# Block attention with decay and a gated FFN on one Trainium2 core: q of the first two batches moves to the casting DMA queue, the first tables are made in another order, and the scores of block 2 stand later in the order

## The chip, the cores and the metric

The kernel runs on one core of a Trainium2 chip. The metric is the device time of one execution in microseconds (us), as a median over several executions. Engines are named as in the profile: PE (TensorE matmul), PEld (its weight loads), DVE (VectorE), ACT (ScalarE), POOL (GpSimd) and SP (SyncE, which here only issues DMAs).

## The reference

Inputs are q, k, v of shape (4 batches, 8 heads, 768 positions, 64), one decay `lam` per head, and three FFN weights (512x1536, 512x1536, 1536x512), all fp32. The reference works in blocks of positions; the kernel uses blocks of 128.

```python
Dmask = np.where(rel >= 0, lam ** rel, 0)                 # inside a block
intra = (qb @ kb.T * Dmask) @ vb
inter = (qb * lam ** (pos + 1)) @ kv_state                # what earlier blocks left
out_block = intra + inter
kv_state = lam ** block * kv_state + (kb * lam ** (block - 1 - pos)).T @ vb
...
x = out (tokens x 512)
result = (sigmoid(x @ w_gate) * (x @ w_val)) @ w_out      # 3072 x 512, fp32
```

## The kernel before

The 768 positions are six blocks n = 0 to 5 of 128 positions; a block holds all four batches, so it is 512 tokens for the FFN. Everything is computed in bf16 with fp32 sums. The order on every engine is the order in which the program writes its instructions: the schedule is by hand.

**Pieces of a block.** `piece_t` gets q and k transposed, two batches at a time. For blocks 0 and 1 PE does it into PSUM (`tq`, `tk`); for blocks 2 to 5 `transpose_by_dma(n)` (line 157) issues two DMA transposes on SP, first q into `QR`, then k into `KR`, and `piece_t` is only `scale_q`. `scale_q` (line 164) is one DVE multiplication that scales q by the table `lamq` (the powers of lam) and writes `QS`. `piece_s` (line 209) forms the scores of the listed batches on PE from `KS` (a view of `KR` from block 2 on) and `QS`, in two PSUM tiles `sp` a batch; `piece_m` (line 217) multiplies one batch's scores by `mask` on DVE (two instructions); `piece_a` (lines 223, 230, 237) makes the attention output on PE and copies it to `XT` on ACT. `make_kd` (line 241) scales k on POOL, and `piece_c` (lines 249, 254, 262) updates the state `Sb`.

**FFN.** `piece_gv(n, ft)` (lines 276, 279, 282, 286) makes one of twelve column tiles: four matmuls into `gp`, a sigmoid on ACT, four matmuls into `vp`, and a DVE product `ht`. `piece_po` (line 296) makes the output, in two halves of six matmuls for each batch.

**Order.** From block 1 on, the order is a list of units: twelve `gv` units and eight `po` halves a block. `place(n, c, t, s, m, a)` hangs the pieces of the next block n behind units. For n = 2 the units are those of block 1's FFN, u = `start[1]`: the transposes behind unit u, `scale_q` of batches 0, 1 behind u+2 and of batches 2, 3 behind u+3, scores behind u+6 and u+9, the attention behind u+10 and u+13. For later blocks, scores stand behind u+4 and u+7.

**Start.** Block 0's q and k of batches 0 and 1 come by the hardware queues as fp32 into the tiles `QF` and `KF` (q on SP after `lam`, k on ACT; line 66). ACT casts k, DVE scales q by the table `qn` while casting it, and `piece_t0(b)` (line 192) transposes q and k of one batch on PE. All other loads are DMAs that cast to bf16, issued by POOL in one row: v of batches 0, 1 (line 85), the first sixth of `WG` and `WV` (`load_gv(0)`, lines 91 and 92), the table `ip1` (line 314), q and k of batches 2, 3, the next sixth of `WG` and `WV` (called WG1 and WV1 below), v of batches 2, 3, the other weights and then blocks 1 and 2. `warm(x)` (line 326) runs x idle matmuls. `load(3)` and later follow `make_kd(2)` on POOL.

**Buffers that matter here.** The `ps_at` pool has five PSUM buffers for `sp`, `op`, `tq`, `tk`, `cp`; `ps_ff` has three for `gp`, `vp`, `po`; `QS` has three.

Of the kernel before, what the change touches and what calls it, by code (L numbers as in the profile page):

```python
# [8 lines left out]
FP32 = mybir.dt.float32  # L9
BF16 = mybir.dt.bfloat16  # L10
AF = mybir.ActivationFunctionType
ALU = mybir.AluOpType
# [4 lines left out]
def kernel(  # L17
# [11 lines left out]
    nc = tc.nc  # L29

    B, H, S, D = q.shape
    C = 128
    NSTEP = S // C
    HP = H // 2
# [5 lines left out]
    NB2 = B // 2  # L40

    const = ctx.enter_context(tc.tile_pool(name="const", bufs=1))
    qkv = ctx.enter_context(tc.tile_pool(name="qkv", bufs=4))
    kdp = ctx.enter_context(tc.tile_pool(name="kdp", bufs=2))
    trsb = ctx.enter_context(tc.tile_pool(name="trsb", bufs=3))
# [3 lines left out]
    osb = ctx.enter_context(tc.tile_pool(name="osb", bufs=4))  # L49
    stp = ctx.enter_context(tc.tile_pool(name="stp", bufs=1))  # L50

    ps_at = ctx.enter_context(tc.tile_pool(name="ps_at", bufs=5, space=bass.MemoryType.PSUM))
# [6 lines left out]
    lam_bc = const.tile([128, H], FP32, tag="lam_bc")  # L59
    nc.sync.dma_start(out=lam_bc, in_=lam.partition_broadcast(128))  # L60

    QF, KF = [], []
    for lst, src, eng in ((QF, q, nc.sync), (KF, k, nc.scalar)):
        for b in range(NB2):
            t = osb.tile([128, H, D], FP32, tag="ob", name="qkf")
            eng.dma_start(out=t, in_=src[b, :, 0:C, :].rearrange("h s d -> s h d"))
            lst.append(t)

    WG = const.tile([128, NMT, DFF], BF16, tag="WG")
    WV = const.tile([128, NMT, DFF], BF16, tag="WV")  # L70
# [5 lines left out]
    Q, K, V = {}, {}, {}  # L76

    def load(n, what, b0, b1):
        sl = slice(n * C, (n + 1) * C)
        for c in what:  # L80
            lst, src = {"q": (Q, q), "k": (K, k), "v": (V, v)}[c]
            if n not in lst:
                lst[n] = qkv.tile([128, B, H, D], BF16, tag=c + "b", name=c + "b")
            t = lst[n]
            nc.gpsimd.dma_start(  # L85
                out=t[:, b0:b1],
                in_=src[b0:b1, :, sl, :].rearrange("b h s d -> s (b h) d"))
# [12 lines left out]
    Sb = stp.tile([128, B, HP, 128], BF16, tag="Sb", name="Sb")  # L100
    nc.vector.memset(Sb, 0.0)  # L101
    ident = const.tile([128, 128], BF16, tag="ident")
    jn = const.tile([128, 3], FP32, tag="jn")
    ip1 = const.tile([128, C], FP32, tag="ip1")
    tri = const.tile([128, C], FP32, tag="tri")
    for c, lst in (("q", Q), ("k", K)):
        lst[0] = qkv.tile([128, B, H, D], BF16, tag=c + "b", name=c + "b")

    for i, (base, m) in enumerate(((1, 1), (-1, -1), (C - 1, -1))):
        nc.gpsimd.iota(jn[:, i:i + 1], pattern=[[0, 1]], base=base, channel_multiplier=m,  # L110
                       allow_small_or_imprecise_dtypes=True)
    load(0, "v", 0, 2)
    make_upper_triangular(nc, tri, val=1.0, diag=True)
    make_identity(nc, ident)

    lnl = const.tile([128, H], FP32, tag="lnl")
    nc.scalar.activation(lnl, lam_bc, AF.Ln)
    qn = const.tile([128, H], FP32, tag="qn")
    nc.scalar.activation(qn, lnl, AF.Exp, scale=jn[:, 0:1])
    pk = const.tile([128, H], FP32, tag="pk")  # L120
    nc.scalar.activation(pk, lnl, AF.Exp, scale=jn[:, 1:2])

    for b in range(NB2):
        nc.scalar.copy(K[0][:, b], KF[b])
        nc.vector.tensor_tensor(out=Q[0][:, b], in0=QF[b],
                                in1=qn.unsqueeze(2).to_broadcast([128, H, D]), op=ALU.mult)
    mask = const.tile([128, HP, 2, C], FP32, tag="mask")
    lnp = const.tile([128, HP], FP32, tag="lnp")
    lamq = const.tile([128, HP, C], BF16, tag="lamq")
    kds = const.tile([128, H], FP32, tag="kds")  # L130
    dec = const.tile([128, HP], FP32, tag="dec")

    def make_mask():
        nc.vector.tensor_tensor(out=mask.rearrange("p g u c -> p (g u) c"),
                                in0=tri.unsqueeze(1).to_broadcast([128, H, C]),
                                in1=pk.unsqueeze(2).to_broadcast([128, H, C]), op=ALU.mult)

    def make_tables():
        for u in range(2):
            us = slice(u * 64, (u + 1) * 64)  # L140
            nc.scalar.activation(lnp[us, :], lam_bc[us, u::2], AF.Ln)
        for hp in range(HP):
            nc.scalar.activation(lamq[:, hp, :], ip1, AF.Exp, scale=lnp[:, hp:hp + 1])
        nc.scalar.activation(kds, lnl, AF.Exp, scale=jn[:, 2:3])
        nc.scalar.activation(dec, lnp, AF.Exp, scale=float(C))
        nc.scalar.preload_act_table_set("sigmoid_and_others")


    QS, KS, MT, XT, KD = {}, {}, {}, {}, {}
# [12 lines left out]
    def scale_q(n, bp, src):  # L162
        t = trsb.tile([128, 2, HP, C], BF16, tag="QS", name="QS")
        nc.vector.tensor_tensor(out=t, in0=src,  # L164
                                in1=lamq.unsqueeze(1).to_broadcast([128, 2, HP, C]), op=ALU.mult)
        for i in range(2):
            QS[n, 2 * bp + i] = t[:, i]
# [16 lines left out]
        for i in range(2):  # L184
            KS[n, 2 * bp + i] = t[:, i]

    def piece_t0(b):

        tt = ps_at.tile([128, 2, HP, C], BF16, name="tt", tag="ps")
        for i, src in enumerate((Q[0], K[0])):  # L190
            for hp in range(HP):
                nc.tensor.transpose(tt[:, i, hp, :], src[:, b, 2 * hp:2 * hp + 2, :], ident)
        t = trsb.tile([128, 2, HP, C], BF16, tag="QS" if b else "KS", name="QK")
        if b == 0:
            nc.vector.tensor_copy(t, tt)
        else:
            nc.scalar.copy(t, tt)
        QS[0, b], KS[0, b] = t[:, 0], t[:, 1]

    SP, OP = {}, {}  # L200

# [37 lines left out]
    def make_kd(n):  # L239
        KD[n] = kdp.tile([128, B, H, D], BF16, tag="kd", name="kd")  # L240
        nc.gpsimd.tensor_tensor(  # L241
            out=KD[n], in0=K[n],
            in1=kds.unsqueeze(1).unsqueeze(3).to_broadcast([128, B, H, D]), op=ALU.mult)

    def piece_c(n, bs):
        for b in bs:
            cp = ps_at.tile([128, HP, 128], FP32, name="cp", tag="ps")
            for hp in range(HP):
                nc.tensor.matmul(cp[:, hp, :], lhsT=KD[n][:, b, 2 * hp:2 * hp + 2, :],  # L249
                                 rhs=V[n][:, b, 2 * hp:2 * hp + 2, :],  # L250
                                 start=(hp == 0), stop=(hp == HP - 1), skip_group_check=True)
            if n > 0:
                sd = kdp.tile([128, HP, 128], FP32, tag="sd", name="sd", bufs=4)
                nc.gpsimd.tensor_tensor(out=sd, in0=Sb[:, b],  # L254
                                        in1=dec.unsqueeze(2).to_broadcast([128, HP, 128]),
                                        op=ALU.mult)
            for u in range(2):
                us = slice(u * 64, (u + 1) * 64)
                if n == 0:
                    nc.vector.tensor_copy(Sb[us, b, :, us], cp[us, :, us])  # L260
                else:
                    nc.vector.tensor_tensor(out=Sb[us, b, :, us], in0=cp[us, :, us],  # L262
                                            in1=sd[us, :, us], op=ALU.add)
# [26 lines left out]
    def piece_po(n, tt, half):  # L290
# [17 lines left out]
        else:  # L308
# [6 lines left out]
                   allow_small_or_imprecise_dtypes=True)  # L315
# [6 lines left out]
    def warm(x):  # L322

        wp = ps_ff.tile([128, TCH], FP32, name="wp", tag="ff")
        for _ in range(x):
            nc.tensor.matmul(wp, lhsT=Sb[:, 0, 0, :], rhs=Sb[:, 0], start=True, stop=True)  # L326


    warm(7)
    piece_t0(0)  # L330
    piece_t0(1)
    make_mask()
    make_tables()
    make_kd(0)
    for i in range(3):
# [39 lines left out]
    def place(n, c, t, s, m, a):  # L375


        for bp in range(2):
            bs = [2 * bp, 2 * bp + 1]
            after[c[bp]].append(lambda bs=bs: piece_c(n - 1, bs))  # L380
            after[t[bp]].append(lambda bp=bp: piece_t(n, bp))
            after[s[bp]].append(lambda bs=bs: piece_s(n, bs))
            after[s[bp]].append(lambda b=bs[0]: piece_m(n, b))
            after[m[bp]].append(lambda b=bs[1]: piece_m(n, b))
        for bp in range(2):
            bs = [2 * bp, 2 * bp + 1]
            after[a[bp]].append(lambda bs=bs: piece_a(n, bs))

    u = proj[0]
    place(1, (u - 2, u - 1), (u + 1, u + 3), (u + 2, u + 4), (u + 3, u + 4), (u + 5, u + 6))  # L390
    for n in range(2, NSTEP):
        u = start[n - 1]
        d = 2 if n == 2 else 0
        place(n, (u, u + 1), (u + 2, u + 3), (u + 4 + d, u + 7 + d), (u + 5 + d, u + 8 + d),
              (u + 8 + d, u + 11 + d))
        after[u].insert(0, lambda n=n: transpose_by_dma(n))
        after[u + 1].append(lambda n=n: make_kd(n))
    for i, u in enumerate(units):
# [36 lines left out]
```

## Time and profile before

| | |
|---|---|
| median of 3 runs | 243.11 us (242.81 to 243.45) |
| profiled execution: its own time | 247.18 us |
| its span (first to last instruction) | 245.4 us |
| PE, DVE, ACT, POOL busy | 226.4, 112.6, 81.1, 84.1 us |
| casting queue (q0): packets, share of 16 DMA engines' span | 77904, 72.3% |
| hardware queue q1 (stores, transposes, q): packets, share | 22464, 18.4% |
| hardware queue q10 (k of batches 0, 1): packets, share | 2080, 1.0% |

The profile is one execution, and it was 4.07 us longer than the median of the timed runs; 1.78 us of it lie outside its span. Busy times of different engines overlap. A page of it has 40 equal slices of the span (6.1 us each here), the chain of work that ended last, groups of instructions by line, and DMA issues; the trace answers for single stretches, tiles and waits.

### The profile page before, as it was taken

The numbers are of one execution on the slowest core, as the hardware profiler recorded it, in microseconds if no ns is written. First come the engines' busy times: TensorE is split into PE (matmuls) and PEld (weight loads), VectorE is DVE, ScalarE is ACT, GpSimd is POOL, SyncE is SP. The second block draws the span as 40 slices with busy tenths as digits, with TensorE's granted clock in tenths as the row PEclk, the third lists the DMA queues.
The fourth block names the chain that finished last, engine by engine and source line by source line (L and its number), as shares of the span: only waits on it lengthen the run. The fifth ranks groups of instructions, "written<-read, shape, count | busy, mean of one in ns | idle before, by whom it ended". The sixth has DMA issues, their size and how long they took to land.

```text
span 245.4 us, 3768 instructions
## 1 busy us (share of the span) xinstructions
PE 226.4 (92%) x1501; PEld 114.5 (47%) x1528; DVE 112.6 (46%) x180; ACT 81.1 (33%) x144; POOL 84.1 (34%) x71
## 2 busy tenths in 40 slices
PE   5598999999977999997999998999999999999993
PEld 1355645565433454443554443554444554444441
DVE  1546345680952740299730299730297720234300
ACT  4374433235220233321431331431332432333221
POOL 8857960499972910099100093000000000000000
PEclk9999999999995899999999999999999999999999
DMA  4999999999999799464992470002470002200022
GB/s 107 193 174 187 197 206 169 157 197 204 140 130 157 51 159 155 129 130 27 157 75 85 123 134 3 0 3 85 118 139 4 0 0 88 85 0 0 3 85 87
DMA packets 102466, 25.42 MB, mean 104 GB/s; under 512 B 91568, under 2 KB 99504, under 8 KB 102448
## 3 DMA queue, kind: packets, MB, share of 16 engines
q0 software_dynamic: 77904, 13.63, 72.3%
q1 hardware_dynamic: 22464, 11.02, 18.4%
q10 hardware_dynamic: 2080, 0.52, 1.0%
q8 instruction: 12, 0.20, 0.3%
q14 instruction: 6, 0.05, 0.1%
HBM read 28.32 MB, written 6.29 MB: 141 GB/s over the span
## 4 chain that ended last, share of the span: by engine, by line
PE 84%; DMA 8%; DVE 2%; SPq 2%; issue 2%; ACT 1%; ACTq 0%; DVEq 0%
PE po L296 25%; PE gp L276 24%; PE vp L282 23%; DMA KR<-kb 5%; DMA qkf<-in_q_dram 3%; PE op L230 3%; PE op L223 2%; PE cp L249 2%; SPq L157 1%; PE wp L326 1%; DVE ht L286 1%; DVE MT L217 1%; ACT XT L237 1%; PE tk L181 1%; PE tq L177 1%
## 5 line engine op out<-in xcount | busy, mean ns | idle before, releaser
L286 DVE TENSOR_TENSOR ht<-sg,vp 128x512 bf16<-128x512 bf16 (+1 forms) x76 | 50.0, 658 | 103.5 <-PE vp L282 98.4
L276 PE MATMUL gp<-XT,WG 128*128 128x512 bf16 (+1 forms) x295 | 75.1, 374 | 3.8 <-DVE ht L286 2.4
L282 PE MATMUL vp<-XT,WV 128*128 128x512 bf16 (+1 forms) x296 | 74.3, 370 | 0.3
L279 ACT ACTIVATE sg<-gp 128x512 bf16<-128x512 f32 (+1 forms) x76 | 43.7, 575 | 90.8 <-PE gp L276 88.1
L296 PE MATMUL po<-WO,ht 128*128 128x512 bf16 x280 | 63.6, 379 | 0.6 <-issue 0.3
L282 PEld LDWEIGHTS <-WV 128*128 128x128 bf16 x304 | 30.1, 99 | 33.4 <-issue 1.6
L276 PEld LDWEIGHTS <-WG 128*128 128x128 bf16 x304 | 28.6, 99 | 33.6 <-issue 6.2
L296 PEld LDWEIGHTS <-ht 128*128 128x128 bf16 x288 | 27.4, 98 | 32.1
L254 POOL TENSOR_TENSOR sd<-Sb,dec 128x512 f32<-128x512 bf16 x16 | 16.9, 1078 | 41.4 <-DVE Sb L262 41.4
L309 ACT COPY ob<-po 128x512 f32<-128x512 f32 x23 | 13.5, 586 | 47.5 <-PE po L296 47.5
L241 POOL TENSOR_TENSOR kd<-kb,kds 128x2048 bf16<-128x2048 bf16 x6 | 22.6, 3773 | 6.5 <-DMA kb<-in_k_dram 6.5
L237 ACT CAST XT<-op 128x512 bf16<-128x512 f32 x24 | 13.0, 589 | 10.9 <-PE op L230 10.9
L262 DVE TENSOR_TENSOR Sb<-cp,sd 64x256 bf16<-64x256 f32 x32 | 13.5, 421 | 0.8
L164 DVE TENSOR_TENSOR QS<-QR,lamq 128x1024 bf16<-128x1024 bf16 x8 | 13.1, 1642 | 0.0
L85 POOL DMA_DIRECT2D vb<-in_v_dram x8 | 11.6, 1450 | 3.4 <-DMA kb<-in_k_dram 1.7
L85 POOL DMA_DIRECT2D qb<-in_q_dram x7 | 10.4, 1488 | 6.2 <-issue 6.2
L85 POOL DMA_DIRECT2D kb<-in_k_dram x7 | 10.2, 1459 | 1.7 <-issue 1.7
L326 PE MATMUL wp<-Sb 128*128 128x512 bf16 x22 | 8.6, 494 | 2.1 <-DVE Sb L101 2.0
L230 PE MATMUL op<-MT,vb 128*64 128x128 bf16 x192 | 8.2, 222 | 0.6 <-DVE MT L217 0.6
L230 PEld LDWEIGHTS <-vb 128*64 128x64 bf16 x192 | 5.8, 109 | 3.2 <-issue 1.8
L209 PEld LDWEIGHTS <-KR 64*128 64x128 bf16 x128 | 3.9, 99 | 6.5 <-DMA KR<-kb 3.6
L223 PEld LDWEIGHTS <-Sb 128*128 128x128 bf16 x80 | 5.3, 98 | 2.4
(143 smaller groups left out, 119.8 us busy)
## 6 DMA issues: line engine op xcount, KB each, us to landing
out_dram<-ob SPq DMA_DIRECT2D x23, 256.0 KB, 2.0
qb<-in_q_dram POOLq DMA_DIRECT2D x4, 512.0 KB, 9.5
kb<-in_k_dram POOLq DMA_DIRECT2D x4, 512.0 KB, 10.7
vb<-in_v_dram POOLq DMA_DIRECT2D x4, 512.0 KB, 12.2
WG<-in_moe_w_gate_dram POOLq DMA_DIRECT2D x6, 256.0 KB, 11.5
WV<-in_moe_w_val_dram POOLq DMA_DIRECT2D x6, 256.0 KB, 11.5
WO<-in_moe_w_out_dram POOLq DMA_DIRECT2D x3, 512.0 KB, 11.3
vb<-in_v_dram POOLq DMA_DIRECT2D x4, 256.0 KB, 13.4
```

The lines of the kernel that those rows point to most:

```text
L85: nc.gpsimd.dma_start(out=t[:, b0:b1], in_=src[b0:b1, :, sl, :].rearrange("b h s d -> s (b h) d"))
L230: nc.tensor.matmul(OP[n, b][us, hp, :], lhsT=V[n][:, b, 2 * hp + u, :], rhs=MT[n, b][:, u, hp, :], start=(n == 0 and hp == 0), stop=(hp == ...
L237: nc.scalar.copy(XT[n][:, :, b, :], OP[n, b])
L241: nc.gpsimd.tensor_tensor(out=KD[n], in0=K[n], in1=kds.unsqueeze(1).unsqueeze(3).to_broadcast([128, B, H, D]), op=ALU.mult)
L254: nc.gpsimd.tensor_tensor(out=sd, in0=Sb[:, b], in1=dec.unsqueeze(2).to_broadcast([128, HP, 128]), op=ALU.mult)
L262: nc.vector.tensor_tensor(out=Sb[us, b, :, us], in0=cp[us, :, us], in1=sd[us, :, us], op=ALU.add)
L276: nc.tensor.matmul(gp[:, :w], lhsT=WG[:, mt, fs], rhs=x[:, mt, :], start=(mt == 0), stop=(mt == NMT - 1))
L279: nc.scalar.activation(sg[:, :w], gp[:, :w], AF.Sigmoid)
L282: nc.tensor.matmul(vp[:, :w], lhsT=WV[:, mt, fs], rhs=x[:, mt, :], start=(mt == 0), stop=(mt == NMT - 1))
L286: nc.vector.tensor_mul(HT[n, ft][:, ts], sg[:, :w], vp[:, :w])
L296: nc.tensor.matmul(po, lhsT=HT[n, ft][:, tt * 128:(tt + 1) * 128], rhs=WO[:, ft, :], start=(ft == 0), stop=(ft == NFT - 1))
L309: nc.scalar.copy(ob, po)
```

## The change

- q of block 0, batches 0 and 1, is no longer loaded as fp32 on SP; it is the first DMA on POOL, with cast, ahead of the small tables. v of these batches comes after the tables. k's two loads stay on hardware queues, now one on ACT's and one on SP's.
- The table `qn` is gone. q of block 0, batches 0 and 1, is transposed on PE as it is (`piece_tq0`) and scaled by `scale_q`, as for all other batches. k is cast by DVE instead of ACT and transposed a batch at a time (`piece_tk0`).
- `lnp` and `lamq` are made on ACT at the very start instead of in `make_tables`. The table `ip1` is made before them; the line that made it between the weight loads stays as well, so `ip1` is written twice.
- `warm(7)` becomes `warm(8)`, and a `warm(2)` stands between the transposes of k and those of q.
- For block 2, `scale_q` moves from u+2 and u+3 to u+6 and u+8, the scores from u+6 and u+9 to u+8 and u+10, the masking along with them, and the attention from u+10 and u+13 to u+11 and u+14.

```diff
-    QF, KF = [], []
-    for lst, src, eng in ((QF, q, nc.sync), (KF, k, nc.scalar)):
-        for b in range(NB2):
-            t = osb.tile([128, H, D], FP32, tag="ob", name="qkf")
-            eng.dma_start(out=t, in_=src[b, :, 0:C, :].rearrange("h s d -> s h d"))
-            lst.append(t)
+    KF = []
+    for b, eng in enumerate((nc.scalar, nc.sync)):
+        t = osb.tile([128, H, D], FP32, tag="ob", name="kf")
+        eng.dma_start(out=t, in_=k[b, :, 0:C, :].rearrange("h s d -> s h d"))
+        KF.append(t)
...
-    for i, (base, m) in enumerate(((1, 1), (-1, -1), (C - 1, -1))):
-        nc.gpsimd.iota(jn[:, i:i + 1], pattern=[[0, 1]], base=base, channel_multiplier=m,
+    load(0, "q", 0, 2)
+    for i, base in enumerate((-1, C - 1)):
+        nc.gpsimd.iota(jn[:, i:i + 1], pattern=[[0, 1]], base=base, channel_multiplier=-1,
                        allow_small_or_imprecise_dtypes=True)
+    nc.gpsimd.iota(ip1, pattern=[[1, C]], base=1, channel_multiplier=0,
+                   allow_small_or_imprecise_dtypes=True)
+    make_identity(nc, ident)
+    make_upper_triangular(nc, tri, val=1.0, diag=True)
     load(0, "v", 0, 2)
-    make_upper_triangular(nc, tri, val=1.0, diag=True)
-    make_identity(nc, ident)
...
-    for b in range(NB2):
-        nc.scalar.copy(K[0][:, b], KF[b])
-        nc.vector.tensor_tensor(out=Q[0][:, b], in0=QF[b],
-                                in1=qn.unsqueeze(2).to_broadcast([128, H, D]), op=ALU.mult)
...
+    def piece_tk0(b):
+        tk = ps_at.tile([128, HP, C], BF16, name="tk", tag="ps")
+        for hp in range(HP):
+            nc.tensor.transpose(tk[:, hp, :], K[0][:, b, 2 * hp:2 * hp + 2, :], ident)
+        KS[0, b] = trsb.tile([128, HP, C], BF16, tag="KS", name="KS")
+        nc.scalar.copy(KS[0, b], tk)
+
+    def piece_tq0():
+        tq = ps_at.tile([128, 2, HP, C], BF16, name="tq", tag="ps")
+        for i in range(2):
+            for hp in range(HP):
+                nc.tensor.transpose(tq[:, i, hp, :], Q[0][:, i, 2 * hp:2 * hp + 2, :], ident)
+        scale_q(0, 0, tq)
...
-    warm(7)
-    piece_t0(0)
-    piece_t0(1)
+    warm(8)
+    nc.vector.tensor_copy(K[0][:, 0], KF[0])
+    piece_tk0(0)
     make_mask()
+    warm(2)
+    nc.vector.tensor_copy(K[0][:, 1], KF[1])
+    piece_tq0()
+    piece_tk0(1)
     make_tables()
...
-        d = 2 if n == 2 else 0
-        place(n, (u, u + 1), (u + 2, u + 3), (u + 4 + d, u + 7 + d), (u + 5 + d, u + 8 + d),
-              (u + 8 + d, u + 11 + d))
+        if n == 2:
+            place(n, (u, u + 1), (u + 6, u + 8), (u + 8, u + 10), (u + 9, u + 11), (u + 11, u + 14))
+        else:
+            place(n, (u, u + 1), (u + 2, u + 3), (u + 4, u + 7), (u + 5, u + 8), (u + 8, u + 11))
```

More of the change, by code (lines that the diff above doesn't have):

```diff
@@ L102 @@
     ident = const.tile([128, 128], BF16, tag="ident")
-    jn = const.tile([128, 3], FP32, tag="jn")
+    jn = const.tile([128, 2], FP32, tag="jn")
     ip1 = const.tile([128, C], FP32, tag="ip1")
     tri = const.tile([128, C], FP32, tag="tri")
-    for c, lst in (("q", Q), ("k", K)):
-        lst[0] = qkv.tile([128, B, H, D], BF16, tag=c + "b", name=c + "b")
-    for i, (base, m) in enumerate(((1, 1), (-1, -1), (C - 1, -1))):
-        nc.gpsimd.iota(jn[:, i:i + 1], pattern=[[0, 1]], base=base, channel_multiplier=m,
+    K[0] = qkv.tile([128, B, H, D], BF16, tag="kb", name="kb")
+    load(0, "q", 0, 2)
+    for i, base in enumerate((-1, C - 1)):
+        nc.gpsimd.iota(jn[:, i:i + 1], pattern=[[0, 1]], base=base, channel_multiplier=-1,
                        allow_small_or_imprecise_dtypes=True)
+    nc.gpsimd.iota(ip1, pattern=[[1, C]], base=1, channel_multiplier=0,
+                   allow_small_or_imprecise_dtypes=True)
+    make_identity(nc, ident)
+    make_upper_triangular(nc, tri, val=1.0, diag=True)
     load(0, "v", 0, 2)
-    make_upper_triangular(nc, tri, val=1.0, diag=True)
-    make_identity(nc, ident)
     lnl = const.tile([128, H], FP32, tag="lnl")
     nc.scalar.activation(lnl, lam_bc, AF.Ln)
-    qn = const.tile([128, H], FP32, tag="qn")
-    nc.scalar.activation(qn, lnl, AF.Exp, scale=jn[:, 0:1])
     pk = const.tile([128, H], FP32, tag="pk")
-    nc.scalar.activation(pk, lnl, AF.Exp, scale=jn[:, 1:2])
-    for b in range(NB2):
-        nc.scalar.copy(K[0][:, b], KF[b])
-        nc.vector.tensor_tensor(out=Q[0][:, b], in0=QF[b],
-                                in1=qn.unsqueeze(2).to_broadcast([128, H, D]), op=ALU.mult)
+    nc.scalar.activation(pk, lnl, AF.Exp, scale=jn[:, 0:1])
+    lnp = const.tile([128, HP], FP32, tag="lnp")
+    for u in range(2):
+        us = slice(u * 64, (u + 1) * 64)
+        nc.scalar.activation(lnp[us, :], lam_bc[us, u::2], AF.Ln)
+    lamq = const.tile([128, HP, C], BF16, tag="lamq")
+    for hp in range(HP):
+        nc.scalar.activation(lamq[:, hp, :], ip1, AF.Exp, scale=lnp[:, hp:hp + 1])
     mask = const.tile([128, HP, 2, C], FP32, tag="mask")
-    lnp = const.tile([128, HP], FP32, tag="lnp")
-    lamq = const.tile([128, HP, C], BF16, tag="lamq")
     kds = const.tile([128, H], FP32, tag="kds")
@@ L138, in make_tables @@
     def make_tables():
[L139 to L144, printed above, removed]
+        nc.scalar.activation(kds, lnl, AF.Exp, scale=jn[:, 1:2])
         nc.scalar.activation(dec, lnp, AF.Exp, scale=float(C))
@@ L185, in piece_t @@
             KS[n, 2 * bp + i] = t[:, i]
-    def piece_t0(b):
-        tt = ps_at.tile([128, 2, HP, C], BF16, name="tt", tag="ps")
-        for i, src in enumerate((Q[0], K[0])):
-            for hp in range(HP):
[L192 to L198, printed above, removed]
+    def piece_tk0(b):
[7 more added lines that the diff above has]
+        for i in range(2):
+            for hp in range(HP):
+                nc.tensor.transpose(tq[:, i, hp, :], Q[0][:, i, 2 * hp:2 * hp + 2, :], ident)
+        scale_q(0, 0, tq)
     SP, OP = {}, {}
```

## The prediction, before the result was known

> **What bounds the kernel now.** I read the page first: PE is busy for 92% of the span, and its clock is granted in full in all slices but two.
>
> ```profile
> span 245.4 us, 3768 instructions
> ...
> PE 226.4 (92%) x1501; PEld 114.5 (47%) x1528; DVE 112.6 (46%) x180; ACT 81.1 (33%) x144; POOL 84.1 (34%) x71
> ...
> PEclk9999999999995899999999999999999999999999
> ```
>
> So a gain must come from where PE stands still or runs slow: the start, and the hole at slices 13 and 14. The waits and the chain say what the hole is (start, duration, what):
>
> ```profile
> PE sp_966 L209 <- DMA KR<-kb: 3.1, 1, 3.1
> ```
>
> ```profile
> 60.08 3.14 SPq L157
> 63.32 11.68 DMA KR<-kb
> 76.08 1.82 PE gp L276 x4
> 77.91 1.28 PE vp L282 x3
> 79.41 1.91 PE gp L276 x4
> 81.32 0.86 PE vp L282 x4
> ```
>
> The k transpose of block 2 lands at 63.32 + 11.68 = 75.00 (other blocks' take 4.8 to 4.9); PE had reached the scores at 71.98 and waits 3.07 us. After it, four matmuls take 1.8 to 1.9 us and not 0.86. The stretches show the clock (PE, PEld, DVE, ACT, POOL busy, clock, DMA share, GB/s):
>
> ```profile
> 72.00:75.00 3.00, 0.00 (x0) 0.00 (x0) 0.69 (x1) 0.00 (x0) 0.05 (x1) 0.90 1.65 98
> 75.00:77.00 2.00, 1.95 (x19) 1.21 (x20) 1.29 (x2) 0.00 (x0) 0.00 (x0) 0.50 2.47 158
> ```
>
> **Price of the hole.** From 71.98 on PE does one set of scores (0.45) and two gv units (4 x 0.86 = 3.44), so it should be through at 75.87; it is at 81.32 + 0.86 = 82.18. The hole costs 6.31 us, half of it wait, half slow clock.
>
> The start, from the timeline:
>
> ```profile
> 9.26 0.69 DVE L125 TENSOR_TENSOR qb<-qkf,qn 128x512 bf16<-128x512 f32 x1 [1.44 <-DMA qkf<-in_q_dram]
> 16.50 0.60 PE L276 MATMUL gp<-XT,WG 128*128 128x256 bf16 x4 [0.25 <-ACT XT L237]
> 19.50 0.74 POOL L91 DMA_DIRECT2D WG<-in_moe_w_gate_dram  x1 [0.66 <-DMA WV<-in_moe_w_val_dram]
> 19.58 0.60 PE L282 MATMUL vp<-XT,WV 128*128 128x256 bf16 x4
> ```
>
> The second q tile lands at 9.23; 7.27 us later the FFN begins. The third row tells more: POOL's issues wait, eight deep, for the landing of the eighth before, so these waits date the landings. WV1 lands at 19.5, and PE first uses it at 19.58: the casting queue is right behind PE.
>
> **What the Trainium skill says.** "TensorE: Matmul & The Clock Gate", Part 1 (The HAM clock gate): an idle window of about 3.4 us takes PE to half clock until a busy window has passed. The trace agrees: clock 0.50 after a wait of 3.07, for some 6 us. "DMA: Bandwidth & Descriptors", section "SWDGE vs HWDGE vs iDMA": a DMA that casts must be issued by GpSimd, and each DMA engine takes its queues in turn. The trace agrees: while KR is on its way (64 to 72 us) q0 moves 3224 packets and q1 2627. "SBUF — State Buffer", section "Who interferes with whom": a DVE instruction with two SBUF inputs and a GpSimd instruction that reads SBUF exclude each other for a whole instruction. The trace agrees: `scale_q`, alone 0.68, took 3.50 beside `make_kd`:
>
> ```profile
> 108.49 4.07 POOL L241 TENSOR_TENSOR kd<-kb,kds 128x2048 bf16<-128x2048 bf16 x1
> 109.60 3.50 DVE L164 TENSOR_TENSOR QS<-QR,lamq 128x1024 bf16<-128x1024 bf16 x1
> ```
>
> **Part 1: block 2 later.** The scores move two units of 1.73 us. Without wait PE reaches them at 71.98 + 3.46 = 75.44, KR has landed at 75.00: margin 0.44. The wait goes, and with it the half clock: minus 6.31. What is late next is DVE. From 75.44: `ht` 75.6 to 76.2, two maskings (0.60 apart) to 77.4, `scale_q` of batches 2, 3 to 78.1, `ht`, two maskings to about 80.3. The second scores come after 75.44 + 0.45 + 3.46 = 79.35 and need four of five `ps_at` buffers; the last one is freed by the first of those maskings, about 79.6. I add 0.3. QS is ready at 78.1, 1.2 earlier. `ht` then comes late but before its PSUM buffer is needed. The first `scale_q` falls at 72.7, when POOL has just ended `sd` (72.05). Bounds for the DVE queue: 0 (the buffers don't bind) to 1.5 (each of four maskings delays PE). The later attention has room: block 2's FFN starts at unit u+20.
>
> **Part 2: the start.** No packet of the casting queue moves before 7.0 (q1 and q10 alone are seen up to there, 248 of q0 from 7 to 8), although v was issued at 1.42. q is now first, issued about 0.6 earlier. Two such loads land 1.67 apart (13.47 to 15.14). So q lands, by estimate, at 7.0 + 1.67 + 0.5 for its end = 9.2 if 7.0 is fixed, 8.6 if the delay counts from the issue. Then PE: 8 + 4 transposes at the slow rate (1.04 for 8: 1.56), `warm(2)` 0.85, and from the scores to the FFN 4.67 as before (11.83 to 16.50): the FFN at q + 7.1, 15.7 to 16.3. `scale_q` (1.04 + 0.69 + about 0.2) and the copy of the k transposes (1.56 + 0.59) lie beside the `warm(2)`. DVE's two casts of k (nearest row: ACT's 0.62) and the mask (1.22) fit between k's landing (about 5.6) and q's. ACT's `lnp` and `lamq` (0.42 + 1.28) leave the path, where they stood ahead of `XT`; PE's own row was as long, so I count nothing for it.
>
> But the start is capped. Before, v landed at 1.42 + 9.1 = 10.5 and WV1 9.0 later. Now q is ahead, v follows at +1.67 and WV1 at +10.7: 19.3 to 19.9. PE wants it at q + 7.1 + 3.08 = 18.8 to 19.4. So WV1 decides, and this point moves by -0.3 to +0.3 from 19.58; with q faster than I think, to -1.5. I take 0.
>
> POOL: the second `ip1` must wait until ACT has read the first, about 4.54 (when `lam` is there) + 0.2 + 0.3 + 0.42 + 1.28 = 6.8. The q and k loads of batches 2, 3 queue behind it and start near 7.1 and not 5.51. The queue then still has v, WG and WV (4.4 us of landings), so this hides; without that cover it would cost up to 1.6. I add 0.2 for it. SP: one load less, nothing behind it. The extra `warm` matmuls lie in PE's wait for q. `qn` and its two multiplications go, off the new path.
>
> **Sum.** Against the profiled execution: 247.18 - 6.31 + 0.3 + 0.2 = 241.4. The timed runs are 4.07 shorter than that execution. Between 28 and 72 us PE has no wait to lose, so I think that the difference lies in the start, the end or the hole; then the hole of the timed runs is worth between 6.31 - 4.07 = 2.2 and 6.31. I take the middle, 4.3: 243.11 - 4.3 + 0.5 = **239.3**. Ends: 236.6 (the whole hole, nothing added), 241.6.
>
> **Rivals.**
> B, a new wait for the same landing. The margin is 0.44, and KR shares the engines with block 3's loads (from 64). If PE comes earlier than the queue, or KR lands 1 to 2 later, PE waits 1 to 2, too short for the clock, and the gain is 2 to 3 less: 241.7. For it speaks 11.68 against 4.9; against it, that SP's issue follows PE (it comes right behind the last store of block 0).
> C, slower: DVE locked out. `make_kd(3)` starts at 78.17, when block 3's k lands; `scale_q` of batches 2, 3 now starts at about 77.4. If k lands more than 0.75 earlier against PE, or PE comes 0.75 later, `scale_q` waits for the whole 3.62, `ht` and the maskings behind it. QS is then there at up to 82.4 where PE wants it at 79.35: a wait of 3.1, as long as the one removed, with the half clock after it. Cost 6.3 where the timed runs had 4.3, plus 0.5: 245.6. Against it: kd starts late in this trace.
> D, nothing: the timed runs have hardly a hole, and the gain goes into the start: 243.
>
> **Chances.** A 0.70 (own range 236.6 to 241.6), B 0.12, C 0.13, D 0.05. No difference means within 0.3%, about what a measurement of this kernel can tell. Faster: A, and most of B, 0.80; same 0.07 (the rest of B, D); slower 0.13. The range 236.4 to 243.6 holds A, B and D.
>
> **What would show it.** Right: no wait of L209 for KR, clock 9 in slices 13 to 15, a first FFN matmul at 15.7 to 16.3, the casting queue first at 6.4 to 7.0, vp of the third tile near 19.6, `scale_q` in 0.7. Wrong: `scale_q` near 77 with 2 us or more; a wait for KR over 1 us; a start over 1 us later; or a span that shrinks by 6 while the timed runs gain under 2, which would say that the hole belongs to the profiled execution.

## The result, and the profile after

The changed kernel takes 239.55 us (median of 4 runs, 239.06 to 241.11) beside 243.28 for the kernel before (242.81 to 243.68): ratio 0.9859, 95% interval 0.9809 to 0.9908. In a later comparison it was 239.60 (6 runs), ratio 0.982 (0.978 to 0.9861). Single executions of the kernel before scatter unusually far, from 242.0 to 247.9, and the two profiles of it have the PE clock down at different places; all ten of the changed kernel lie between 239.06 and 241.11. The ratios leave out every execution over 1.5% above the fastest of its kernel.

The forecast was 239.3 with a range of 236.4 to 243.6. The total is right; the experiments show that neither of its two parts has the size that was forecast.

The page of the changed kernel:

```profile
span 238.0 us, 3771 instructions
...
PE 224.2 (94%) x1504; PEld 113.6 (48%) x1531; DVE 111.0 (47%) x180; ACT 79.8 (34%) x142; POOL 84.8 (36%) x72
...
PEclk9799999999999999999999999999999999999999
```

The span is 7.4 us shorter, not 3.7: the first profile of before was a long execution. The dip of the clock at slices 13 and 14 is gone; one at slice 2 is new. The stretches that held the hole (PE, PEld, DVE, ACT, POOL busy, clock, DMA share, GB/s):

```profile
72.00:75.00 3.00, 3.00 (x28) 1.42 (x26) 1.53 (x3) 1.19 (x2) 0.00 (x0) 1.00 3.17 153
75.00:77.00 2.00, 1.95 (x13) 0.91 (x11) 2.00 (x4) 0.60 (x1) 0.00 (x0) 1.00 4.10 149
```

PE is busy throughout at full clock. The timeline of the start and of block 2's pieces:

```profile
8.11 1.01 PE L193 MATMUL tq<-ident,qb 128*128 128x128 bf16 x8 [1.73 <-DMA qb<-in_q_dram]
14.96 0.60 PE L272 MATMUL gp<-XT,WG 128*128 128x256 bf16 x4
19.07 0.61 PE L278 MATMUL vp<-XT,WV 128*128 128x256 bf16 x4 [0.72 <-DMA WV<-in_moe_w_val_dram]
...
74.48 0.62 PE L205 MATMUL sp<-QS,KR 64*128 64x128 bf16 x16
76.45 0.68 DVE L158 TENSOR_TENSOR QS<-QR,lamq 128x1024 bf16<-128x1024 bf16 x1
77.25 3.62 POOL L237 TENSOR_TENSOR kd<-kb,kds 128x2048 bf16<-128x2048 bf16 x1 [5.71 <-DMA kb<-in_k_dram]
78.59 0.62 PE L205 MATMUL sp<-QS,KR 64*128 64x128 bf16 x16
```

q lands at 8.1 and the FFN begins at 14.96, and then PE waits 0.72 for WV1, the landing that the prediction named as the cap. The dip at slice 2 falls between q and the FFN:

```profile
8.20:11.60 3.40, 3.40 (x27) 1.93 (x29) 1.31 (x3) 2.00 (x4) 3.40 (x5) 0.50 1.60 177
```

The scores of block 2 do not wait for k's transpose. `scale_q` starts 0.80 us before `make_kd`, and 0.28 before it in the second profile (76.55 and 76.83): that is the margin to the collision of rival C.

The span divides into three stretches, by the first FFN matmul of blocks 1 and 2 in the timelines:

| | FFN of block 0 from | FFN of block 1 from | block 1 takes | from block 2 to the end |
|---|---|---|---|---|
| before, first profile | 16.50 | 58.84 | 41.62 | 144.94 |
| before, second profile (first experiment) | 17.59 | 59.92 | 37.27 | 144.95 |
| changed | 14.96 | 57.95 | 35.53 | 144.47 |
| changed, second profile | 14.90 | 58.04 | 35.53 | 144.5 |

Against the first profile 0.89 comes from the start, 6.09 from block 1 and 0.47 from the end; against the second, 1.97, 1.74 and 0.48.

### The profile page after: what moved, and what is told of

Read it like the earlier page. It is cut to its first block, busy times and chain, and to the rows that moved or that the text cites. A ratio compares the mean times of both kernels' runs of the same rounds, so it can differ in the third digit from the quotient of the medians.

```text
span 238.0 us, 3771 instructions
## 1 busy us (share of the span) xinstructions
PE 224.2 (94%) x1504; PEld 113.6 (48%) x1531; DVE 111.0 (47%) x180; ACT 79.8 (34%) x142; POOL 84.8 (36%) x72
## 4 chain that ended last, share of the span: by engine, by line
PE 87%; DMA 4%; POOL 3%; issue 2%; DVE 2%; ACT 0%; ACTq 0%; POOLq 0%; DVEq 0%
PE po L292 26%; PE gp L272 26%; PE vp L278 26%; DMA WV<-in_moe_w_val_dram 4%; PE op L226 3%; PE sp L205 2%; PE cp L245 2%; PE op L219 2%; DVE MT L213 1%; DVE ht L282 1%; POOL WG L90 1%; POOL qb L84 1%; POOL kb L84 0%; POOL vb L84 0%; PE tk L175 0%
## 5 line engine op out<-in xcount | busy, mean ns | idle before, releaser
L272 PE MATMUL gp<-XT,WG 128*128 128x512 bf16 (+1 forms) x294 | 73.3, 368 | 3.3 <-DVE ht L282 2.4
L278 PEld LDWEIGHTS <-WV 128*128 128x128 bf16 x304 | 29.6, 98 | 33.5 <-DMA WV<-in_moe_w_val_dram 1.0
L213 DVE TENSOR_TENSOR MT<-sp,mask 128x512 bf16<-128x512 f32 x48 | 30.5, 682 | 3.5 <-PE sp L205 3.5
L250 POOL TENSOR_TENSOR sd<-Sb,dec 128x512 f32<-128x512 bf16 x16 | 16.2, 1042 | 35.4 <-DVE Sb L258 35.4
L84 POOL DMA_DIRECT2D qb<-in_q_dram x8 | 11.8, 1474 | 6.4 <-issue 5.6
L158 DVE TENSOR_TENSOR QS<-QR,lamq 128x1024 bf16<-128x1024 bf16 x8 | 12.1, 1514 | 0.0
L322 PE MATMUL wp<-Sb 128*128 128x512 bf16 x25 | 9.3, 475 | 2.1 <-DVE Sb L100 2.0
```

Of the source, the lines that this page charges most:

```text
L84: nc.gpsimd.dma_start(out=t[:, b0:b1], in_=src[b0:b1, :, sl, :].rearrange("b h s d -> s (b h) d"))
L213: nc.vector.tensor_tensor(out=MT[n, b][:, u], in0=SP[n, b][u], in1=mask[:, :, u], op=ALU.mult)
L250: nc.gpsimd.tensor_tensor(out=sd, in0=Sb[:, b], in1=dec.unsqueeze(2).to_broadcast([128, HP, 128]), op=ALU.mult)
L272: nc.tensor.matmul(gp[:, :w], lhsT=WG[:, mt, fs], rhs=x[:, mt, :], start=(mt == 0), stop=(mt == NMT - 1))
L278: nc.tensor.matmul(vp[:, :w], lhsT=WV[:, mt, fs], rhs=x[:, mt, :], start=(mt == 0), stop=(mt == NMT - 1))
```

## The experiments

The theory to start with (1) was the prediction's: the gain is the hole at block 2. The rival (2): it is made at the start. Code lines differ a little between the kernels, so go by the names of the tiles.

### The kernel before once more

> The kernel before, unchanged, for a second profile. Theory 1 (the hole at block 2 belongs to the kernel): again a wait of L209 for KR of 2 to 3 us behind unit u+6; its timed runs lie near 243.2. If the half clock after it is what made the first profiled execution 4 us longer than the timed runs, this profile has the wait without the half clock, or with less of it, and a span near 241.5. Theory 2 (the hole belonged to that one execution): no wait over 1 us, span 239 to 240 with the same start.

Its profile (own time 243.96) has the wait without the half clock after it:

```profile
PE sp L209 <- DMA KR<-kb: 1.2, 1, 1.2
```

Instead the clock was down at the start (same columns as above):

```profile
8.70:15.50 6.80, 5.44 (x35) 2.39 (x37) 4.91 (x7) 4.17 (x10) 4.36 (x6) 0.50 2.05 173
```

Half clock for 6.8 us made the FFN begin at 17.59. The span, 242.1, was near the 241.5 that theory 1 gave. So the hole is there in both profiles, but costs 1.74 in one and 6.09 in the other; the difference is the half clock that came after a wait of 3.07 and not after one of 1.24. Its five timed runs were 243.96 and four of 246.54 to 247.54, which gives a ratio of 1.0155 (1.0085 to 1.0225) to the very same program: with few runs, differences of 1.5% in either direction say little here. Every execution of the changed kernel (ten, 241.11 at most) is nevertheless faster than every one of the kernel before (more than a hundred, 241.98 at least).

### Each part alone

Block 2 alone is the kernel before with the new `place` line of n = 2; the start alone is the changed kernel with the old lines:

```diff
-        if n == 2:
-            place(n, (u, u + 1), (u + 6, u + 8), (u + 8, u + 10), (u + 9, u + 11), (u + 11, u + 14))
...
+        d = 2 if n == 2 else 0
+        place(n, (u, u + 1), (u + 2, u + 3), (u + 4 + d, u + 7 + d), (u + 5 + d, u + 8 + d),
+              (u + 8 + d, u + 11 + d))
```

> Before with only the placement of block 2 changed. Theory 1: minus 3 to 4 us (239.3 to 240.3), no wait for KR over 0.5 us, block 2's FFN starts at 100.46 minus about 6 in the profile against the first profile of before. Theory 2 (the gain is made at the start): within 1 us of before (242.3 to 243.5).

> The changed kernel with block 2's placement as before. Theory 1: minus 0 to 1 us (242.3 to 243.3): PE is 0.9 earlier at 28 us, but the k transposes of block 2 land no earlier than the DMA queues let them, so the wait grows by what the start gains. Theory 2: minus 3 us or more (240.3 or less).

Measured: block 2 alone 0.9933 (0.9909 to 0.9957), the start alone 0.9875 (0.9849 to 0.99). Of 243.9 us these are 1.6 and 3.0. The means of all executions, 243.60 and 242.14 beside 244.92, say nearly the same (1.3 and 2.8). Both theories fail in their pure form; the start is the larger part, where theory 1 gave it 0 to 1. In the profile of the start alone the FFN of block 1 begins at 57.73, PE still waits 1.47 for KR, and block 1 takes 37.07. The product of the two ratios is 0.981, so together they give what the changed kernel gives (0.982, 0.9859).

Block 2 alone shows rival C at work (timeline):

```profile
76.36 3.62 POOL L241 TENSOR_TENSOR kd<-kb,kds 128x2048 bf16<-128x2048 bf16 x1 [4.97 <-DMA kb<-in_k_dram]
77.35 3.17 DVE L164 TENSOR_TENSOR QS<-QR,lamq 128x1024 bf16<-128x1024 bf16 x1
80.58 0.45 PE L209 MATMUL sp<-QS,KR 64*128 64x128 bf16 x9 [1.02 <-DVE QS L164]
```

Here `make_kd` came 0.99 before `scale_q`, which then took 3.17 and not 0.68. The second scores waited 1.02 for it and 0.75 for a masking behind it; block 1 took 37.59.

### Scale_q one unit later: the price of the collision

```diff
-            place(n, (u, u + 1), (u + 6, u + 8), (u + 8, u + 10), ...
+            place(n, (u, u + 1), (u + 6, u + 9), (u + 8, u + 10), ...
```

> The changed kernel with scale_q of batches 2, 3 of block 2 one unit later (behind u+9), so that it comes due on DVE about 1.6 after make_kd of block 3 has started on POOL. Lock theory (DVE's two SBUF inputs against POOL's read, rival C of the prediction): scale_q takes 2 us or more and ends with make_kd, near 81 to 81.5; the second scores wait 2 to 3 us; plus 1.5 to 3 us of time against the changed kernel (241 to 242.5). If the lock does not matter: scale_q in 0.7, ready about 79.5 where the scores want it at 78.6, so a wait of 0.9 and plus 0.5 to 1 us.

```profile
77.61 3.62 POOL L237 TENSOR_TENSOR kd<-kb,kds 128x2048 bf16<-128x2048 bf16 x1 [6.83 <-DMA kb<-in_k_dram]
77.81 3.97 DVE L158 TENSOR_TENSOR QS<-QR,lamq 128x1024 bf16<-128x1024 bf16 x1
81.83 1.04 PE L205 MATMUL sp<-QS,KR 64*128 64x128 bf16 x16 [4.21 <-DVE QS L158]
```

```profile
82.00:86.00 4.00, 4.00 (x24) 1.78 (x21) 1.66 (x3) 0.60 (x1) 4.00 (x3) 0.50 1.12 72
```

The lock theory holds, and the wait is larger than it said: 4.21, and the clock falls to half afterwards. Block 1 takes 42.63 in this profile, which was one of the longer executions of this kernel (245.83; twenty took 241.78 to 246.98), so 42.63 is not its usual price. The ratio to the kernel before is 1.0003 (0.9967 to 1.0038): one DVE instruction one unit later takes back the whole gain of the change, 1.5 to 1.9% by the ratios. The Trainium skill, "SBUF — State Buffer", section "Who interferes with whom", says that the second of the two blocks for the whole of the first; the trace agrees: `make_kd` ended at 81.23 and `scale_q` 0.55 later, about its own length.

### Scale_q early again

Two kernels with `scale_q` of block 2 behind u+2 and u+3 and the scores late: the changed kernel so (first), and the kernel before with block 2 alone so (second).

```diff
-            place(n, (u, u + 1), (u + 6, u + 8), (u + 8, u + 10), ...
+            place(n, (u, u + 1), (u + 2, u + 3), (u + 8, u + 10), ...
```

> The changed kernel with block 2's scale_q back behind u+2 and u+3, scores and all else late as changed. Lock theory: scale_q now runs beside POOL's sd (1 us each) and not near make_kd, costs 0.7 to 1.5 with PE unharmed, and no execution can fall into the collision with make_kd; same time as the changed kernel in its good executions (239.0 to 239.7) and fewer runs of 241 and more. If the late scale_q had a use of its own: 0.5 us or more slower than the changed kernel.

> The kernel before with only block 2's scores, masks and attention moved as in the change, scale_q left behind u+2 and u+3. In the run with the whole block 2 change and the old start, scale_q was locked out by make_kd and the second scores waited 1.02 and 0.75. Lock theory: here no such wait, block 1's twelve gv and eight po units take 35.5 us as in the changed kernel and not 37.6, and the time is 1 to 2 us below that run's, near 240.5 to 241.5. Otherwise: the same 37.6 and no gain over it.

First: 239.59 us, ratio 0.983 (0.9786 to 0.9874), block 1 takes 35.54. It equals the changed kernel; the late `scale_q` has no use of its own. Second: block 1 takes 35.54 and no score waits, as the lock theory said, but the ratio is 0.9935 (0.9904 to 0.9965), the same as that of block 2 alone. So the collision is shown in a profile and taken away; that it costs time in most executions of the former kernel is not. One difference stands out: nine of the 22 executions of block 2 alone took 245.4 or more, and none of the 14 with `scale_q` early took more than 243.61. No profile of one of the nine was kept, and the two kernels were timed in different comparisons, so whether the collision makes them is not shown.

### Block 3's loads later: why k's transpose was late

The kernel before, with POOL held up ahead of block 3's loads:

```diff
             if i == start[n - 1]:
+                if n == 3:
+                    for _ in range(4):
+                        nc.gpsimd.memset(scr, 0.0)
                 load(n, "qkv", 0, B)
```

> The kernel before, with four POOL memsets of an unused 128x2048 fp32 tile ahead of block 3's loads, so that these begin some 4 to 9 us later and the transposes of block 2 have the DMA engines to themselves. Sharing theory (k's transpose is late because block 3's loads share the engines with it): KR lands within 5 to 6 us of its issue, at 68 to 69.5; the scores behind u+6 do not wait; block 1 takes 35.5 us as in the changed kernel; time like the two kernels with block 2 moved alone, 0.3 to 0.8% below before. If the transposes are slow by themselves: the wait stays at 1.2 to 3.1 and the time within 0.3% of before.

The loads begin at 68.89, and KR lands 5.2 after its issue at 63.05 (11.7 in the first profile of before):

```profile
61.55 7.39 POOL L404 MEMSET scr<- 128x2048 f32 x4
68.89 1.74 POOL L85 DMA_DIRECT2D qb<-in_q_dram  x1
```

```profile
DMA to landing us min/median/max: 5.2/5.2/5.2
```

The scores, still behind u+6, have no wait for KR, and block 1 takes 35.53. Ratio 0.9887 (0.9786 to 0.9987). The sharing theory holds: the hole was block 3's loads on the same DMA engines, and either later scores or later loads close it. By the profile that is clear; the ratio rests on four runs.

### More on the hardware queues: what the start gains

The changed kernel with two idle fp32 loads of 256 KB added to the hardware queues:

```diff
+    for b, eng in enumerate((nc.scalar, nc.sync)):
+        t = osb.tile([128, H, D], FP32, tag="ob", name="xf")
+        eng.dma_start(out=t, in_=q[b, :, 0:C, :].rearrange("h s d -> s h d"))
```

> The changed kernel with two more fp32 loads of 256 KB on the hardware queues (the two q tiles of before, which nothing reads), so that these carry as much as before the change. Backlog theory (the casting queue does not begin while the hardware queues are full): the first casting packet at 6.5 to 7.0 as before, q lands at 9.5 to 10.5, WV1 at 20 to 21. Issue theory (it begins 3.0 after POOL's first issue whatever else runs; the 7.0 of before had another cause): first packet at 4.3, q at 8.5 to 9.5.

The packets of the casting queue in the first 7 us, in the changed kernel and then in this one:

```profile
q0 software_dynamic: 2305, 0.29, 65.6%
```

```profile
q0 software_dynamic: 23, 0.00, 0.7%
```

```profile
PE tq L196 <- DMA qb<-in_q_dram: 4.0, 1, 4.0
```

The backlog theory holds: 23 packets instead of 2305, with POOL's issue at 1.26 in both. q landed at 11.1, three us later than in the changed kernel and later than the 9.5 to 10.5 expected, and the FFN began at 18.48, 7.4 after q as the prediction's row of PE work has it (7.1). Block 1's FFN began at 60.81 instead of 57.95, the end took 144.95 again, and this one execution took 243.06 us. Block 1's FFN is then later than in both profiles of before (58.84 and 59.92), although q still avoids a multiplication and a table. So what the start gains hangs on half a megabyte less on the hardware queues, behind which the casting queue does not begin; how much of its gain in time that is, one execution can't say.

### More warm matmuls in the kernel before

`warm(7)` made `warm(13)`, so that PE has no hole from 5 to 7.9.

> The kernel before with warm(13) in place of warm(7), so that PE has no hole from 5 to 7.9. Clock theory (half of what the start gains is that the clock stays up; the second profile of before had half clock from 8.7 to 15.5 and its FFN began at 17.6): full clock at the start, FFN at 15.5 to 16.5, and time 0.5 to 1.5 us below before, no more, since WV1 still lands at 19.5. Queue theory (only q's landing and WV1 matter): within 0.3 us of before.

```profile
5.00:10.50 5.50, 3.67 (x24) 1.72 (x23) 1.99 (x4) 1.55 (x4) 5.48 (x7) 1.00 1.67 208
10.50:14.00 3.50, 3.28 (x23) 1.24 (x22) 3.23 (x5) 3.27 (x10) 2.10 (x3) 0.51 1.96 174
```

The clock still fell, at 10.5 for 3.5 us; the FFN began at 16.55 and block 1's at 58.88, as in the first profile. Ratio 1.0019 (0.999 to 1.0048): no gain. More `warm` matmuls alone do nothing here. But the kernel did not get the full clock that the clock theory asked for, so what a start at full clock is worth was not tested, nor whether the change's own `warm(8)` and `warm(2)` help to keep it: in five of seven profiles with the new start the clock did not fall before the FFN.

### One write of ip1, and both mendings

The changed kernel without the second `ip1`, and the same with `scale_q` early:

```diff
     load_gv(0, DFF // 6)
-    nc.gpsimd.iota(ip1, pattern=[[1, C]], base=1, channel_multiplier=0,
-                   allow_small_or_imprecise_dtypes=True)
     load(0, "qk", 2, 4)
```

> The changed kernel without the second write of ip1. Prediction's step (0.2 at most): time within 0.3 us of the changed kernel (239.3 to 239.9); POOL issues q of batches 2 and 3 about 0.4 earlier (6.75 and not 7.11), and the third tile's vp starts at the same 19.1, set by WV1. If the POOL queue counts, vp starts 0.3 or more earlier and so does everything up to block 2.

> The changed kernel with both mendings: ip1 written once, and block 2's scale_q behind u+2 and u+3. If both hold: 238.6 to 239.3, at or below the kernel with one ip1 alone (239.08), and below the changed kernel by 0.3 to 0.8 us. If neither does: equal to the changed kernel within 0.3 us.

The first issues q of batches 2, 3 at 6.75 and not 7.11, its third vp is at 18.26 and not 19.07, and the span is 237.2. That is not the doing of the second write: with `scale_q` one unit later, which writes `ip1` twice, the third vp is at 18.03, and with both mendings it is at 19.19. Timed, it is 239.08 (4 runs; ratio 0.9826, 0.9774 to 0.9877). The second kernel is 239.54 (7 runs; 0.982, 0.9774 to 0.9865) beside 239.60 for the changed kernel in the same comparison:

> The changed kernel once more, beside the two mended ones on the same chip. 239.0 to 241.2 as before, with more runs near 241 if make_kd and scale_q (0.8 us apart in its first profile) sometimes collide.

All six runs of the latter lay between 239.28 and 239.84; the runs near 241 that were expected did not come. In the profile of the kernel with both mendings PE waited at four places between 8 and 19.2 and the clock fell at 19.0 for 3.4 us, so that block 1 began at 59.52: its early FFN (13.69) only met the same queue. No version beats the changed kernel by what can be measured.

## Why the prediction was right, and where it was not

**Total: right, by luck: two errors cancel.** It gave the hole 4.3 of the timed runs and the start a loss of 0.2. Measured alone they are 1.6 and a gain of 3.0. Its ends, 236.6 and 241.6, come out of its own terms as 243.11 - 6.31 = 236.8 and 243.11 - 2.24 + 0.5 = 241.4; nothing hangs on that. The sign that the hole belongs to the profiled execution was half met: the span shrank by 7.4 us and the timed runs gained 3.7, of which block 2 alone gives 1.6.

**The hole.** The mechanism was right step by step: KR late because block 3's loads share the engines (the later loads show it), a half clock after the wait, both gone when the scores move. In the first profile the forecast of 6.31 meets a measured 6.09. Mis-sized was the term for the timed runs, "the middle, 4.3" between 2.2 and 6.31: it let the timed runs keep half of what only the one profiled execution had. The second profile of before has 1.74, the kernel with `warm(13)`, after a wait of 1.70, has 1.77 (37.30 for block 1), and block 2 alone gains 1.6: the lower end was near. The difference of 4.07 between profile and timed runs could have been put down to the half clock, which comes or does not; block 1 takes 4.35 more in the first profile than in the second.

**DVE behind the scores.** Added 0.3. The second scores do come 0.2 late (4.11 after the first, where 0.45 + 3.46 = 3.91 was the least), with an early `scale_q` too; but block 1 takes 35.53, as in the kernel with later loads, whose scores stand behind u+6 and u+9, so nothing of it is left in the time.

**The start.** The step that failed is that q lands at "9.2 if 7.0 is fixed, 8.6 if the delay counts from the issue". The casting queue began 3.0 after its issue, near 4.3, since less stood on the hardware queues; the added loads put it back to 6.6. q therefore landed at 8.1.

The row of PE work after q (6.9 against 7.1) came out right at half clock only. In the five other profiles with the new start and no added loads PE kept full clock there, and the FFN began at 13.69 to 13.77, 5.6 after q. With the old start PE was slow somewhere between 7.8 and 15.5 in every profile. That holds for the first profile of before too, although its page has full clock there: four transposes took 0.61 us, and 0.40 in the second profile before its clock fell:

```profile
7.87 0.61 PE L192 MATMUL tt<-ident,qb 128*128 128x128 bf16 x4 [2.71 <-DVE qb L125]
```

```profile
7.91 0.40 PE L192 MATMUL tt<-ident,qb 128*128 128x128 bf16 x4 [2.75 <-DVE qb L125]
```

The cap was right: in all seven profiles with the new start and no added loads PE waits 0.72 or 0.73 for WV1 before the third vp. That stands at 18.03 to 19.19, where 19.3 to 19.9 was given, so most of an early FFN is spent in waiting. What follows was not foreseen: from the third vp to block 1's FFN it takes 38.88 or 38.89 us in six of these seven profiles, and 39.25 or 39.26 in all six with the old start. There the scores of batches 2, 3 wait 0.23 for ACT's copy of k; with the added loads both the wait and the 39.25 are back.

Block 1's FFN thus began at 58.82 to 59.92 with the old start and at 56.91 to 59.52 with the new one, on average 1.3 us earlier. With 0.46 at the end that is 1.8 of the 3.0 measured for the start alone. Thirteen profiled executions are few beside the timed ones; the rest stays open.

**The second ip1.** Forecast 0.2, because it "hides". The third vp stands at 18.03 to 19.15 in five profiles with it and at 18.26 and 19.19 in two without; in time no difference is shown either.

**The end.** Nothing was forecast; 0.47 came (see below).

**Rivals.** B (a new, shorter wait for KR) did not come. C (DVE locked out) is real: its margin was put at 0.75 and is 0.80 and 0.28 in the two profiles, and its place and cause were right. Its price, 6.3 by the profile, is 7.1 (42.63 against 35.53) in the one long execution where it was forced; the timed runs of that kernel came back to the time of before, not to the 245.6 given. It did not happen in the two profiles of the changed kernel.

## What to carry to other kernels

A wait that PE reaches late in one profile can be short in most executions: take a second profile before a single hole is given a price, above all where a half clock hangs on its length. A full clock on the page is not yet full speed, as the start of the first profile shows (0.61 against 0.40 us for the same four transposes): compare the durations of like instructions. Loads on the hardware queues can hold back the whole casting queue, as here from 4.3 to 6.6 us, so what is gained by taking a load off them is an earlier start of everything behind. Before a DVE instruction with two SBUF inputs is moved, look what POOL does at that time: a margin of 0.3 to 0.8 us stood between the gain and its loss.

## What was not expected of the hardware

- **The casting queue did not begin while the hardware queues were full, and shared with them once it had begun.** First packets near 4.3 with 0.5 MB on the hardware queues, near 7 with 1 MB, for issues at 1.26 to 1.42. In both cases the first ones come as q10 runs empty, with q1 still moving, and they come in numbers only as q1 runs empty too (from about 5 and 8). With nothing on them (block 3's loads, held back to 68.89) the first packets came 2.4 after the issue. At block 2 of the changed kernel, block 3's loads were issued at 62.39, and from 64 to 67 only the transpose moved:

```profile
q1 hardware_dynamic: 2082, 0.52, 96.6%
```

  In the first profile of before the transpose's queue ran empty at 64.75 (one packet up to 66.0). The loads began there, then shared almost evenly (3224 packets to 2627 from 64 to 72), and KR took 11.7 instead of 9.6. The Trainium skill, "DMA: Bandwidth & Descriptors", section "SWDGE vs HWDGE vs iDMA", has each DMA engine take its queues in turn; that describes the second case and not the first. What holds the queue back is not shown.
- **The clock can fall without a long wait.** In the kernel before with `warm(13)`, PE was busy for 3.67 of the 5.5 us up to 10.5, with no wait over 1.55, and still had half clock from there to 14.
- **The end is 0.47 shorter with fewer hardware loads.** From block 2 to the end, kernels with the q tiles on hardware queues take 144.93 to 144.95; those with the new start 144.47 to 144.52; and with two idle loads added to the new start it is 144.95 again. The time lies behind the issue of the last store, 3.36 before the end in the first profile of before and 2.89 in the changed kernel; why is open.
